# Sigmoid attention feeding a gated two-layer MLP: another opening, and the table of steps that goes with it

## The chip, the core and the metric

The kernel runs on one core of a Trainium2 chip. A core has engines that run side by side, each through its own list of instructions in order: TensorE (PE; its weight loads are shown as PEld) for matmuls, VectorE (DVE), ScalarE (ACT), GpSimd (POOL) and SyncE (SP). Engines wait for one another through semaphores. Transfers between the chip's main memory and the core's on-chip memory are issued by an engine and carried out by 16 DMA engines. Matmul results go to PSUM, eight banks of accumulators, from which VectorE or ScalarE must take them before a bank is used again. The metric is the time of one execution on the device, in microseconds (us).

## The reference

Two layers follow one another. Attention with a sigmoid in place of a softmax, over 8 images of 448 tokens with 12 heads of 64, and then an MLP over all 3,584 tokens with 768 channels and 2,048 hidden units:

```python
scores = scale * np.matmul(q, k.transpose(0, 1, 3, 2)) - np.log(S)
attn = 1.0 / (1.0 + np.exp(-scores))
x = np.matmul(attn, v)            # then heads side by side: (3584, 768)
h = x @ w_in
g = h * (1.0 / (1.0 + np.exp(-beta * h)))
out = g @ w_out
```

## The kernel before

**Tiling.** The 12 heads of an image are done in three groups of four heads (`QPB` = 3), so there are 24 groups; group `g` belongs to image `g // 3`. Queries and keys of a group are loaded as fp32 and cast to fp16 by the transfer (`load_one`, line 129), into one of three buffers called homes; `RAW_HOMES` (line 65) names the home of each group in the order of loading, `OUT_HOMES` (line 66) the homes of result tiles. VectorE turns queries and keys (`transpose`, line 212): one instruction for queries, two for keys. TensorE computes scores with 32 channels at a time in four strips of its array (`score`, line 236), ScalarE takes the sigmoid out of PSUM (`weigh`, line 248), TensorE multiplies by v in two halves of its columns (`attend`, line 302), and VectorE casts the result to the token tile `xT` (line 335).

**MLP.** Hidden units are computed as matmuls of 128 x 128 weights with 224 or 448 tokens. For image 0 the first units are computed one by one (`dense1`, line 348); the rest, and all of the later images, in seven products per block of a scheme that needs seven multiplications for eight (`wino1`, line 463), with sums of weights (`weight_sum`, line 424) and of tokens (`token_sum`, line 443) made by VectorE. The second layer does the same over pairs of token tiles (`wino2`, line 565; sums of hidden units by `hidden_sum`, line 552). GpSimd multiplies part of the hidden units by their sigmoid (`weigh_right`, line 524, and `weigh_below`, line 534).

**The order is written out by hand.** `OPENING` (line 773) and `STEPS` (line 707) are lists of steps that `follow` (line 695) carries out one after another, and every engine gets its instructions in that order. The letters are keys of `RUN` (line 656). Those that the change and the prediction speak of:

- `lG.r.s` loads half `s` of the queries (`r` = 0) of group G; `kG` its keys; `QG` both, whole; `vB` and `KB` load v of image B; `wC` loads piece C of eight of w_in (256 hidden units), `oC.H` a quarter of w_out. All of these are DMAs that GpSimd issues, on one queue; at most eight are outstanding, since each uses one of eight semaphores again.
- `rG.s` turns half `s` of a group's queries, `RG.0` all queries, `RG.1` the keys; `b` turns beta; `EB` copies the last rows of v within the chip. VectorE does these.
- `hG.s.p` is a half visit: scores of half `s` of the queries with the first (`p` = 0) or second half of the keys, and their sigmoids. `VG.j` is a whole visit. `yG.s` and `zG.s` are the two stages of the attend of a half, `AG` the attend of a group.
- `fD` is unit block D of image 0 for the first half of the tokens, `D0.D` for the second half; `IB.d.p` is product p of the seven for image B; `Xb.i` token sums, `Si.p` and `Ti.p` weight sums; `GB.d` and `BB.d.j` are GpSimd's products.
- `Ot.h.p` and `Ut.p.x` are pieces of the second layer, `Ht.i` sums of hidden units.
- `iN` is N matmuls on zeros that fill TensorE while it waits at the start.

Where the next attend is nearer than the next visit, dense matmuls are issued as two of 64 columns instead of one of 128 (`tiled`, line 702). A visit needs score tiles in PSUM that ScalarE has emptied: three exist up to step `p0`, two behind it. Four banks serve everything else, the one least lately used first (`bank`, line 107).

Ahead of `OPENING` come the loads of group 0's first half of queries and its keys on SyncE's queue, ten fill matmuls, and the turns of these (lines 785 to 848).

Of the kernel before, what the change touches and what calls it, by code (L numbers as in the profile page):

```python
# [13 lines left out]
def kernel(  # L14
# [680 lines left out]
    def follow(steps):  # L695
# [26 lines left out]
        U2.5.0 X2.0 U2.5.1 A8 V9.1 K4 U2.3.0 H4.0 U2.3.1 H4.1 U4.1.0 R11.0 U2.7.0 V9.2  # L722
        U4.1.1 R11.1 U2.7.1 U4.6.0 U4.6.1 Q13 V9.0 E3 U2.4.0 U2.4.1 H4.2 R10.0 H4.3 R10.1
        U4.5.0 U4.2.0 U4.5.1 U4.2.1 X2.1 X2.3 U4.7.0 U4.7.1 U4.3.0 X2.2 V10.0 U4.3.1 I2.0.6
        U4.4.0 U4.4.1 A9 V10.3 I2.0.5 R12.1 I2.0.2 I2.1.1 I2.1.6 I2.0.3 V10.1 I2.1.2 I2.0.7
        I2.1.5 G2.0 I2.1.7 I2.0.4 I2.1.3 V10.2 I2.1.4 Q15 G2.1 R13.1 I2.2.1 B2.0.0 I2.2.6
        A10 B2.1.0 B2.0.1 V11.0 I2.2.2 B2.1.1 I2.2.5 R13.0 I2.2.7 I2.3.1 I2.2.3 V11.1 I2.2.4
        B2.2.0 I2.3.6 B2.2.1 I2.3.5 G2.2 I2.3.2 I2.3.7 U6.1.0 I2.3.3 V11.2 I2.3.4 R12.0 X3.0
        U6.1.1 B2.3.1 A11 B2.3.0 V12.2 X3.1 H6.0 U6.2.0 H6.1 Q14 U6.2.1 X3.3 I3.0.1 V12.0
        H6.2 I3.0.6 E4 X3.2 G2.3 I3.0.5 U6.6.0 R15.1 U6.6.1 H6.3 V12.1 U6.5.0 U6.5.1 I3.0.2  # L730
        I3.0.7 V12.3 I3.0.3 U6.3.0 R14.0 I3.0.4 U6.7.0 U6.7.1 U6.3.1 A12 B3.0.1 R15.0 B3.0.0
# [148 lines left out]
```

## Time and profile before

| | us |
|---|---|
| three runs, median | 366.39 |
| lowest and highest of the three | 365.99, 366.56 |
| the profiled execution, on the same scale | 367.32 |
| its span, first to last instruction | 365.6 |
| TensorE busy in the span | 358.9 |
| VectorE busy | 279.6 |
| ScalarE busy | 250.5 |
| GpSimd busy | 168.9 |

All rows of the profile that follow come from that one execution. Times are counted from the start of its span. A row of the timeline has start, length, engine, line, operation, output tile `<-` input tiles, shapes, a count of merged instructions, and in brackets the idle time of that engine before it with what ended it. A matmul's length includes the time until its results have drained, so the distance from one start to the next is the better measure of what a step costs TensorE. The granted clock of TensorE was 1.000 over the span.

### The profile page before, as it was taken

The page shows a single profiled execution, that of the slowest core. Times are in us where ns is not written, and L with a number is a line of the kernel's source. Part 1 is how long each engine was busy: PE and PEld are TensorE (multiplying, and loading weights), DVE is VectorE, ACT ScalarE, POOL GpSimd, SP SyncE. Part 2 cuts the span into 40 slices and gives each one's busy share as a digit, 9 for nine tenths or more (in the row PEclk, how much of TensorE's full clock was granted, in tenths as well). Part 3 has the DMA queues.
Part 4 walks back from the last instruction along what each step waited for, and adds up shares of the span by engine and source line. Part 5 has one row for each costly group of instructions (what it writes and reads, how often), then busy time and mean ns, then how long its engine had stood idle before and what let it go on. Part 6 is the DMA issues. An engine that isn't in the chain of part 4 may idle for free.

```text
span 365.6 us, 9439 instructions
## 1 busy us (share of the span) xinstructions
PE 358.9 (98%) x3819; PEld 241.0 (66%) x3819; DVE 279.6 (76%) x528; ACT 250.5 (69%) x414; POOL 168.9 (46%) x204
## 2 busy tenths in 40 slices
PE   7989999999999999999999999999999999999996
PEld 2568654587456785676766676657855688878564
DVE  5439969999977789776787876778768568888755
...
DMA  8999999930995213153977810694001210110235
GB/s 165 168 198 201 195 204 206 209 61 10 159 180 131 31 23 52 34 105 68 105 123 98 145 45 2 138 127 90 0 4 29 60 45 2 43 29 19 48 81 174
...
## 3 DMA queue, kind: packets, MB, share of 16 engines
...
q1 hardware_dynamic: 6160, 11.71, 12.6%
...
q14 instruction: 14, 0.11, 0.1%
...
## 4 chain that ended last, share of the span: by engine, by line
PE 88%; DMA 6%; POOL 3%; DVE 1%; issue 1%; ACT 0%; POOLq 0%; DVEq 0%; ACTq 0%
PE m_ps L192 70%; PE sco L239 10%; PE av_ps L321 8%; DMA raw<-in_q_dram 3%; DMA raw<-in_k_dram 2%; POOL gt L540 2%; DMA v<-in_v_dram 1%; POOL raw L133 0%; DVE sum L406 0%; POOL gt L530 0%; DVE qT L217 0%; ACT osb L459 0%; DVE v L167 0%; POOL w_in L174 0%; ACT sg L459 0%
## 5 line engine op out<-in xcount | busy, mean ns | idle before, releaser
L251 ACT ACTIVATE attnT<-sco 128x896 f16<-128x896 f32 (+1 forms) x163 | 139.0, 908 | 41.0 <-PE sco L239 40.3
L406 DVE TENSOR_TENSOR osb<-m_ps,osb 128x448 f32<-128x448 f32 (+2 forms) x217 | 127.3, 597 | 49.0 <-PE m_ps L192 35.6
L540 POOL TENSOR_TENSOR gt<-osb,sg 128x448 f16<-128x448 f32 x60 | 68.4, 1157 | 65.3 <-ACT sg L459 65.3
L192 PEld LDWEIGHTS <-w_in 128*128 128x128 f16 (+1 forms) x942 | 76.9, 101 | 14.0 <-issue 7.5
L192 PE MATMUL m_ps<-xT,w_in 128*128 128x224 f16 (+1 forms) x708 | 73.1, 259 | 1.3 <-DMA w_in<-in_moe_w_in_dram 1.2
L530 POOL TENSOR_TENSOR gt<-osb,sg 128x448 f16<-128x448 f32 x30 | 34.5, 1154 | 81.3 <-ACT sg L459 54.1
L459 ACT ACTIVATE sg<-osb,beta_sb 128x448 f32<-128x448 f32 (+1 forms) x120 | 62.5, 576 | 9.3 <-DVE osb L406 8.5
L192 PEld LDWEIGHTS <-sum 128*128 128x128 f16 (+1 forms) x488 | 40.3, 101 | 26.9 <-issue 4.6
L192 PEld LDWEIGHTS <-w_S 128*128 128x128 f16 (+1 forms) x630 | 51.0, 101 | 9.4 <-issue 5.5
L192 PEld LDWEIGHTS <-gt 128*128 128x128 f16 (+1 forms) x434 | 36.2, 100 | 26.3 <-issue 8.5
L192 PE MATMUL m_ps<-w_out,gt 128*128 128x384 f16 (+2 forms) x314 | 53.1, 323 | 0.0
L239 PE MATMUL sco<-qT,kT 32*128 32x448 f16 (+3 forms) x864 | 51.6, 339 | 0.8 <-DVE kT L832 0.5
L192 PE MATMUL m_ps<-xs,w_S 128*128 128x224 f16 (+1 forms) x408 | 42.3, 259 | 0.0
L192 PE MATMUL m_ps<-w_out,sum 128*128 128x384 f16 (+1 forms) x256 | 41.2, 327 | 0.0
L192 PE MATMUL m_ps<-w_T,sum 128*128 128x384 f16 (+1 forms) x232 | 40.4, 326 | 0.2 <-DVE sum L406 0.2
L335 DVE CAST xT<-av_ps 128x448 f16<-128x448 f32 (+1 forms) x54 | 28.2, 564 | 13.2 <-PE av_ps L321 12.9
L321 PE MATMUL av_ps<-attnT,v 128*64 128x448 f16 (+3 forms) x400 | 38.2, 343 | 0.0
L459 ACT ACTIVATE osb<-m_ps,beta_sb 128x224 f32<-128x224 f32 x56 | 22.1, 450 | 16.0 <-PE m_ps L192 10.5
L321 PEld LDWEIGHTS <-v 128*64 128x64 f16 (+1 forms) x432 | 21.2, 108 | 16.8 <-issue 9.5
L239 PEld LDWEIGHTS <-kT 32*128 32x128 f16 (+1 forms) x864 | 13.5, 96 | 22.5 <-issue 19.5
L192 PE MATMUL m_ps<-xT,w_S 128*128 128x224 f16 (+1 forms) x222 | 22.3, 260 | 0.0
L192 PE MATMUL m_ps<-xs,w_in 128*128 128x224 f16 (+1 forms) x234 | 22.1, 260 | 0.0
...
## 6 DMA issues: line engine op xcount, KB each, us to landing
...
raw<-in_k_dram POOLq DMA_DIRECT2D x23, 224.0 KB, 5.2
raw<-in_q_dram POOLq DMA_DIRECT2D x21, 224.0 KB, 3.7
v<-in_v_dram POOLq DMA_DIRECT2D x32, 144.0 KB, 5.9
w_in<-in_moe_w_in_dram POOLq DMA_DIRECT2D x8, 384.0 KB, 11.3
...
v<-in_v_dram POOLq DMA_DIRECT2D x16, 48.0 KB, 6.0
...
```

Of the source, the lines that this page charges most:

```text
L192: nc.tensor.matmul(to[c : c + step], hidden[:, c : c + step], weights, **({} if step == P else {"tile_position": (0, c)}), **flags,)
L239: nc.tensor.matmul(sco[base : base + nk, hh, u0 : u0 + n], kT[g][lo : lo + BLK, jt * P : jt * P + nk, e], qT[g][lo : lo + BLK, c0 : c0 + n ...
L251: nc.scalar.activation(out=at[:, :, 0:n], in_=sco[:, :, 0:n], func=AF.Sigmoid, bias=NEG_LOG_S, scale=MSCALE,)
L321: nc.tensor.matmul(av[hh * D : (hh + 1) * D, 0:n], vs[b][base : base + nk, 2 * (s % NPAIR) + hh, jt], at[base : base + nk, hh, 0:n], start ...
L335: nc.vector.tensor_copy(out=xTs[b][:, s % NPAIR, c0 : c0 + n], in_=av[:, 0:n])
L406: nc.vector.tensor_tensor(out=out, in0=in0, in1=in1, op=op)
L459: nc.scalar.activation(out=out, in_=in_, func=AF.Sigmoid, bias=0.0, scale=beta_sb[:, dc : dc + 1])
L530: nc.gpsimd.tensor_tensor(out=gt[:, 2 * d : 2 * d + 2, off : off + QH], in0=ob[:, 0], in1=sg, op=ALU.mult)
L540: nc.gpsimd.tensor_tensor(out=gt[:, dc, off : off + S].rearrange("p (h n) -> p h n", h=2), in0=oa[:, :, j], in1=sg, op=ALU.mult,)
```

## The change

Three strings of the kernel are replaced; no function is changed. The opening in full:

```diff
-        l1.0.0 h0.0.0 k1 b0 l2.0.0 i4 r1.0 k2 R1.1 h0.0.1 v0 R2.1 l0.0.1 i4 l1.0.1 h1.0.1 i4
-        w0 w1 w2 r2.0 h1.0.0 i2 i2 h2.0.1 E0 w3 i3 h2.0.0 r0.1 y0.0 z0.0 h0.1.0 r1.1 y1.0
-        l2.0.1 z1.0 h0.1.1 y2.0 z2.0 w4 p0 h1.1.0 Q3 w5 f1 f0 f3 r2.1 I0.2.1 h1.1.1 y0.1
-        z0.1 I0.3.1 h2.1.0 y1.1
+        l2.0.0 l0.0.1 h0.0.0 l1.0.0 i4 k2 k1 v0 w2 r1.0 h0.0.1 l1.0.1 r0.1 l2.0.1 i4 r2.0
+        h0.1.0 R2.1 R1.1 w1 w0 i4 h0.1.1 E0 i2 h1.0.1 i2 i2 h1.0.0 y0.0 z0.0 b0 h2.0.0 y0.1
+        z0.1 w3 r1.1 h2.0.1 y1.0 z1.0 p0 h1.1.0 y2.0 z2.0 Q3 I0.2.1 r2.1 f3 h1.1.1 I0.2.2 f1
+        f0 I0.3.1
```

The second half of group 0's queries is the second load of GpSimd's queue (it was the eleventh), ahead of the first half of group 1's queries and ahead of both keys; its two visits come third and fourth, and its attend second. w_in comes in the order 2, 1, 0, 3 and then 4 to 7, with the second halves of groups 1 and 2 behind piece 2 and group 3 ahead of piece 4. There are 28 fill matmuls for 29.

The table of steps holds the same 864 steps with `OPENING`, in another order. Its start, and the stretch from the attend of group 6 to U2.6.0:

```diff
-        R3.0 z1.1 I0.3.2 I0.2.2 w6 h2.1.1 w7 Q4 X0.0 f9 f2 y2.1 z2.1 X0.1 X0.3 f8 D0.10 D0.9
-        R3.1 o0.0 K1 D0.1 D0.0 D0.2 Q5 S1.1 S2.1 V3.1 D0.11 D0.8 D0.3 S3.1 V3.2 I0.2.6
-        I0.2.5 o1.0 V3.3 X0.2 f11 R4.1 R4.0 o0.1 V3.0 S4.1 I0.2.7 Q6 f10 I0.3.6 V4.1 I0.2.3
...
-        A6 V7.1 T3.1 I1.2.1 I1.3.7 X1.3 G1.3 I1.2.6 I1.2.5 Q11 V7.0 I1.3.4 T2.1 I1.2.2
-        B1.3.1 I1.0.1 I1.2.3 B1.3.0 I1.2.7 G1.2 V7.2 I1.0.6 I1.0.5 I1.2.4 R9.0 I1.0.7 I1.0.2
-        B1.2.0 B1.2.1 I1.0.3 I1.1.1 G1.0 I1.0.4 B1.0.0 I1.1.6 B1.0.1 Q10 I1.1.5 I1.1.2
-        I1.1.7 I1.1.3 V8.0 I1.1.4 B1.1.0 T1.1 A7 B1.1.1 V8.1 R9.1 U2.1.0 U2.1.1 H2.0 H2.1
-        I2.0.1 T4.0 Q12 V8.2 U2.2.0 T1.0 U2.2.1 U2.6.0 K3 H2.2 U2.6.1 H2.3 V8.3 G1.1 T4.1
...
-        U26.3.1 U26.4.1 U26.2.0
+        R3.1 w4 h2.1.0 f2 w5 I0.3.2 y1.1 w6 z1.1 h2.1.1 f9 y2.1 z2.1 R3.0 f8 X0.0 D0.0 X0.1
+        w7 X0.3 D0.8 Q4 o0.0 D0.10 D0.1 D0.11 S1.1 S2.1 V3.1 K1 D0.2 D0.9 Q5 o1.0 D0.3 R4.0
+        X0.2 V3.2 I0.2.6 V3.3 S3.1 I0.2.5 f11 V3.0 R4.1 o0.1 S4.1 Q6 I0.2.7 f10 I0.3.6 V4.1
...
+        V6.3 I1.3.3 R8.0 K3 A6 V7.1 I1.3.7 R9.1 I1.2.1 X1.3 I1.2.6 I1.2.5 G1.3 V7.0 R11.1
+        I1.3.4 T2.1 I1.2.2 I1.0.1 B1.3.1 I1.2.3 I1.0.6 G1.2 B1.3.0 V7.2 I1.2.7 I1.0.2 I1.0.5
+        I1.2.4 I1.0.7 B1.2.0 I1.0.3 I1.1.1 I1.0.4 B1.2.1 I1.1.6 B1.0.0 I1.1.5 R8.1 I1.1.7
+        B1.0.1 G1.0 I1.1.2 I1.1.3 V8.0 I1.1.4 Q15 T1.1 R11.0 A7 B1.1.1 B1.1.0 V8.1 U2.1.0
+        U2.1.1 H2.0 H2.1 R9.0 I2.0.1 T1.0 V8.2 U2.2.0 U2.2.1 T4.1 U2.6.0 G1.1 V8.3 U2.6.1
...
+        U26.7.1 U22.4.1 U26.3.0 U26.3.1 U26.4.0 U26.4.1 U26.2.1
```

The strings of homes follow the new order of loading and of results:

```diff
-    RAW_HOMES = "012012012012012102121010"
+    RAW_HOMES = "012021021021202021010210"
```

`OUT_HOMES` is replaced in the same way.

More of the change, by code (lines that the diff above doesn't have):

```diff
@@ L720 @@
-        I1.1.7 I1.1.3 V8.0 I1.1.4 B1.1.0 T1.1 A7 B1.1.1 V8.1 R9.1 U2.1.0 U2.1.1 H2.0 H2.1
-        I2.0.1 T4.0 Q12 V8.2 U2.2.0 T1.0 U2.2.1 U2.6.0 K3 H2.2 U2.6.1 H2.3 V8.3 G1.1 T4.1
[L722 to L731, printed above, removed]
@@ new lines @@
+        O0.0.0 o1.1 V4.2 R5.0 O1.0.1 O0.0.1 O1.0.2 B0.2.0 O0.0.2 I0.3.4 V4.3 Q7 O1.0.3
+        B0.3.0 A4 V5.1 B0.3.1 R6.0 O0.0.3 O0.0.4 O1.0.4 O0.0.5 S2.0 O1.0.5 O1.1.0 X1.0 V5.2
+        O1.1.1 O0.1.0 O1.0.6 K2 O1.0.7 O0.1.1 V5.0 O1.1.2 O0.0.6 O0.1.2 O0.1.3 R6.1 S4.0
+        O0.0.7 O1.1.3 T3.0 V6.2 T2.0 O1.1.4 Q8 O0.1.4 R7.0 Q9 A5 X1.1 V6.1 S3.0 R7.1 O1.1.5
+        O1.1.6 O0.1.5 O1.1.7 O0.1.6 I1.3.1 X1.2 V6.0 Q11 I1.3.6 E2 I1.3.5 O0.1.7 I1.3.2 T3.1
+        V6.3 I1.3.3 R8.0 K3 A6 V7.1 I1.3.7 R9.1 I1.2.1 X1.3 I1.2.6 I1.2.5 G1.3 V7.0 R11.1
@@ new lines @@
+        I1.3.4 T2.1 I1.2.2 I1.0.1 B1.3.1 I1.2.3 I1.0.6 G1.2 B1.3.0 V7.2 I1.2.7 I1.0.2 I1.0.5
+        I1.2.4 I1.0.7 B1.2.0 I1.0.3 I1.1.1 I1.0.4 B1.2.1 I1.1.6 B1.0.0 I1.1.5 R8.1 I1.1.7
+        B1.0.1 G1.0 I1.1.2 I1.1.3 V8.0 I1.1.4 Q15 T1.1 R11.0 A7 B1.1.1 B1.1.0 V8.1 U2.1.0
+        U2.1.1 H2.0 H2.1 R9.0 I2.0.1 T1.0 V8.2 U2.2.0 U2.2.1 T4.1 U2.6.0 G1.1 V8.3 U2.6.1
+        U2.5.0 H2.3 U2.5.1 A8 H4.0 H4.1 V9.1 Q10 U2.3.0 T4.0 X2.0 U4.1.0 U2.3.1 V9.0 U4.6.0
+        U4.1.1 R10.1 H2.2 Q12 U4.5.0 U4.6.1 U4.2.0 U4.2.1 X2.1 E3 R10.0 H4.3 U2.7.0 U4.5.1
@@ new lines @@
+        U2.7.1 H4.2 V9.2 U4.3.0 U2.4.0 X2.3 X2.2 U4.7.0 R12.0 U4.7.1 U4.3.1 V10.0 U2.4.1
+        I2.0.6 U4.4.0 U4.4.1 A9 Q13 V10.3 I2.1.1 I2.0.5 R12.1 I2.1.6 I2.0.2 I2.0.3 G2.0
+        V10.1 K4 I2.1.5 I2.1.7 I2.1.2 I2.0.7 I2.1.3 V10.2 I2.1.4 B2.1.0 I2.0.4 B2.1.1 B2.0.0
+        I2.2.1 A10 V11.0 B2.0.1 I2.2.6 I2.2.5 I2.2.2 R13.0 G2.1 I2.2.7 I2.2.3 I2.3.1 I2.2.4
+        V11.1 B2.2.1 I2.3.2 E4 B2.2.0 I2.3.6 G2.2 I2.3.5 I2.3.7 U6.1.0 I2.3.3 V11.2 I2.3.4
+        B2.3.1 B2.3.0 U6.1.1 A11 K5 R15.1 H6.0 V12.2 H6.1 U6.2.0 I3.0.1 U6.2.1 X3.0 H6.2 Q14
@@ new lines @@
+        V12.0 U6.5.0 X3.1 U6.6.0 X3.2 G2.3 U6.6.1 U6.5.1 R13.1 Q17 I3.0.6 I3.0.2 I3.0.5 H6.3
+        V12.1 X3.3 I3.0.7 I3.0.3 U6.3.0 U6.3.1 V12.3 H8.0 G3.0 I3.1.1 I3.0.4 A12 V13.1 R15.0
+        U6.7.0 I3.1.6 H8.1 U6.7.1 I3.1.2 I3.1.5 V13.0 Q16 R14.1 U6.4.0 R14.0 I3.1.7 U6.4.1
+        I3.1.3 V13.2 I3.1.4 U8.6.0 G3.1 B3.0.1 B3.1.1 U8.1.0 U8.1.1 A13 V14.2 U8.6.1 H8.2
+        I3.2.1 E5 U8.2.0 U8.5.0 U8.5.1 B3.1.0 V14.0 H8.3 I3.2.6 U8.2.1 U8.3.0 B3.0.0 I3.2.5
+        I3.2.2 I3.2.7 I3.2.3 G3.2 V14.1 R16.0 I3.2.4 U8.7.0 I3.3.1 Q18 U8.3.1 B3.2.1 U8.7.1
@@ new lines @@
+        B3.2.0 I3.3.6 V14.3 I3.3.5 U8.4.0 I3.3.7 I3.3.2 U8.4.1 I3.3.3 I3.3.4 X4.0 U10.1.0
+        B3.3.0 U10.1.1 B3.3.1 A14 X4.1 R16.1 H10.0 H10.1 V15.2 U10.2.0 U10.2.1 I4.0.1 X4.2
+        G3.3 I4.0.6 V15.0 I4.0.5 K6 Q19 H10.2 U10.6.0 X4.3 I4.0.2 U10.6.1 H10.3 I4.0.3 V15.1
+        U10.5.0 I4.0.7 G4.0 R17.1 U10.5.1 V16.2 I4.0.4 R18.1 A15 V16.1 U10.3.0 U10.3.1
+        I4.1.1 H12.2 I4.1.6 U10.7.0 V16.0 U10.7.1 I4.1.5 R18.0 I4.1.7 I4.1.2 R17.0 I4.1.3
+        U10.4.0 U10.4.1 H12.0 G4.1 V16.3 I4.1.4 B4.0.1 E6 B4.1.0 I4.2.1 A16 V17.2 B4.0.0
@@ new lines @@
+        I4.2.6 B4.1.1 I4.2.5 I4.2.2 I4.2.7 I4.2.3 V17.0 I4.2.4 I4.3.1 B4.2.1 H12.1 G4.2
+        R19.1 U12.1.0 I4.3.6 U12.1.1 I4.3.5 U12.6.0 Q20 U12.6.1 I4.3.2 Q21 B4.2.0 U12.2.0
+        H12.3 I4.3.7 I4.3.3 V17.1 R19.0 I4.3.4 U12.2.1 B4.3.0 B4.3.1 U12.5.0 U12.7.0 V18.0
+        U12.5.1 G4.3 X5.0 A17 X5.1 Q22 V18.1 U12.7.1 U12.3.0 U12.3.1 X5.3 V18.2 U12.4.0
+        H14.0 I5.0.1 I5.0.6 U12.4.1 H14.1 U14.1.0 I5.0.5 V18.3 I5.0.2 X5.2 U14.1.1 U14.6.0
+        I5.0.3 U14.6.1 R20.0 G5.0 U14.2.0 R21.0 A18 V19.2 H14.2 U14.2.1 I5.1.1 I5.0.7
@@ new lines @@
+        U14.5.0 I5.1.6 H14.3 V19.1 R20.1 U14.5.1 Q23 R21.1 I5.0.4 I5.1.2 I5.1.5 V19.0
+        U14.3.0 I5.1.7 I5.1.3 U14.3.1 I5.1.4 R22.1 U14.7.0 B5.1.1 B5.1.0 U14.7.1 A19 V20.0
+        R22.0 G5.1 I5.2.1 I5.2.6 U14.4.0 I5.2.5 U14.4.1 V20.2 I5.2.2 I5.3.1 B5.0.1 I5.2.3
+        I5.3.6 V20.1 I5.3.5 I5.2.7 I5.3.7 I5.3.2 I5.3.3 G5.2 K7 B5.0.0 I5.3.4 I5.2.4 V20.3
+        R23.1 X6.0 H16.2 B5.2.0 I6.0.1 B5.2.1 A20 V21.2 X6.1 U18.1.0 U18.1.1 U16.1.0 I6.0.6
+        B5.3.0 U16.1.1 B5.3.1 U18.2.0 I6.0.5 R23.0 V21.0 U16.2.0 U16.2.1 I6.0.2 H16.0
@@ new lines @@
+        U18.2.1 H16.1 E7 I6.0.3 V21.1 G5.3 U16.6.0 U16.6.1 U16.5.0 U16.5.1 H18.0 H16.3
+        U16.7.0 V22.0 U16.7.1 A21 H18.1 V22.2 U16.4.0 U16.3.0 X6.2 U16.3.1 V22.1 I6.1.1 X6.3
+        U18.6.0 I6.0.7 U18.6.1 V22.3 U16.4.1 I6.0.4 I6.1.2 I6.1.6 A22 V23.0 U18.5.0 H18.3
+        I6.1.5 U18.5.1 H18.2 G6.0 V23.2 I6.3.1 U18.3.0 I6.1.3 U18.3.1 V23.1 I6.1.7 I6.3.6
+        B6.0.0 U18.7.0 I6.1.4 I6.2.1 B6.1.1 I6.3.2 I6.3.5 A23 B6.0.1 I6.2.6 I6.2.5 I6.2.2
+        B6.1.0 G6.1 I6.3.7 I6.2.7 I6.2.3 I6.3.3 I6.3.4 U18.7.1 G6.3 I6.2.4 I7.1.1 I7.0.1
@@ new lines @@
+        B6.2.1 B6.3.0 U20.1.0 B6.2.0 G6.2 X7.0 I7.3.1 B6.3.1 U18.4.0 X7.1 I7.1.6 I7.0.6
+        U20.1.1 I7.3.6 I7.3.5 I7.1.2 U18.4.1 X7.2 I7.0.5 H20.0 I7.3.2 I7.0.2 H20.1 I7.1.5
+        X7.3 I7.3.3 U20.5.0 U20.2.0 I7.1.3 H20.2 U20.6.0 U22.1.0 I7.1.7 I7.0.3 U20.6.1 G7.1
+        I7.2.1 I7.2.6 G7.0 I7.1.4 I7.2.5 I7.3.7 U20.7.0 U20.5.1 G7.3 H20.3 U20.2.1 I7.3.4
+        B7.3.0 H22.2 U24.1.0 I7.0.7 U22.1.1 B7.1.1 U20.3.0 I7.0.4 B7.3.1 I7.2.7 U20.7.1
+        U20.3.1 I7.2.2 H22.0 B7.1.0 H22.1 I7.2.3 U22.7.0 I7.2.4 U22.5.0 U22.6.0 B7.2.0
@@ L771 @@
+        U22.2.0 B7.0.0 B7.0.1 U24.1.1 U22.6.1 U22.5.1 H24.2 H22.3 U22.7.1 U26.1.0 U20.4.0
+        B7.2.1 U20.4.1 U24.7.0 G7.2 U22.3.0 U22.2.1 H24.0 U22.3.1 U24.2.0 U24.5.0 H24.1
+        U26.1.1 U24.6.0 U24.6.1 U24.5.1 U26.2.0 H24.3 U24.2.1 H26.0 U24.7.1 U22.4.0 U24.3.0
+        H26.1 U24.3.1 U26.6.0 U26.6.1 U26.5.0 U24.4.0 H26.2 U24.4.1 U26.7.0 H26.3 U26.5.1
+        U26.7.1 U22.4.1 U26.3.0 U26.3.1 U26.4.0 U26.4.1 U26.2.1
     """.split()
     OPENING = """
-        l1.0.0 h0.0.0 k1 b0 l2.0.0 i4 r1.0 k2 R1.1 h0.0.1 v0 R2.1 l0.0.1 i4 l1.0.1 h1.0.1 i4
```

49 lines of the change are left out of this document (3 added, 46 removed).

## The prediction

> **What bounds the kernel now.** I read the page first: shares of the engines, the DMA row, the chain of waits.
>
> ```profile
> span 365.6 us, 9439 instructions
> PE 358.9 (98%) x3819; PEld 241.0 (66%) x3819; DVE 279.6 (76%) x528; ACT 250.5 (69%) x414; POOL 168.9 (46%) x204
> ...
> DMA  8999999930995213153977810694001210110235
> ...
> PE 88%; DMA 6%; POOL 3%; DVE 1%; issue 1%; ACT 0%; POOLq 0%; DVEq 0%; ACTq 0%
> ```
>
> TensorE is 98% busy, so a new order of the same matmuls can only move the 6.7 us in which it is idle, and fill. The DMA row is full to about 72 us, and the chain lies 6% on DMA. So I asked next for the engines' busy time by stretch, cut at steps that I place below (columns: stretch, its length, busy time and count of PE, PEld, DVE, ACT, POOL, granted clock, DMA share, GB/s).
>
> ```profile
> 8.98:18.74 9.76, 9.69 (x156) 4.94 (x157) 3.83 (x11) 8.92 (x13) 7.95 (x12) 1.00 1.38 167
> 18.74:28.84 10.10, 8.77 (x140) 6.26 (x140) 3.72 (x11) 8.45 (x17) 4.26 (x6) 1.00 1.37 200
> 28.84:45.03 16.19, 16.15 (x206) 12.62 (x207) 15.84 (x36) 13.95 (x25) 6.61 (x11) 1.00 1.42 199
> ...
> 71.04:87.97 16.93, 16.93 (x192) 14.05 (x190) 15.80 (x28) 15.64 (x30) 9.67 (x10) 1.00 0.30 59
> ...
> 94.20:361.61 267.41, 267.41 (x2748) 182.50 (x2749) 206.95 (x377) 171.39 (x289) 112.58 (x125) 1.00 0.41 71
> ```
>
> From 94.20 on TensorE has no gap in 267.41 us: nothing can be won there, only lost. It loses 1.33 us between 18.74 and 28.84, where it waits for loads, and next to nothing up to 45.03, but there VectorE is busy 15.84 of 16.19: two engines are full at once. Before 18.74 ScalarE is the full one (8.92 of 9.76).
>
> **The opening, and which loads it waits for.** The timeline, for the steps in question (start, length, engine, line, operation; in brackets the idle time before it and what ended it):
>
> ```profile
> 8.34 0.58 DVE L225 STREAM_TRANSPOSE kT<-raw 128x384 f32<-128x384 f32 x1 [0.16 <-DMA raw<-in_k_dram]
> ...
> 8.98 0.70 PE L239 MATMUL sco<-qT,kT 32*128 32x224 f16 x16 [0.24 <-DVE kT L225]
> ...
> 17.64 1.08 PE L321 MATMUL av_ps<-attnT,v 128*64 128x224 f16 x16
> ...
> 18.74 0.58 PE L239 MATMUL sco<-qT,kT 32*128 32x224 f16 x16
> ...
> 19.63 0.83 POOL L174 DMA_DIRECT2D w_in<-in_moe_w_in_dram  x1 [1.27 <-DMA w_in<-in_moe_w_in_dram]
> ...
> 21.39 0.75 PE L192 MATMUL m_ps<-xT,w_in 128*128 128x224 f16 x6 [0.24 <-DMA w_in<-in_moe_w_in_dram]
> ...
> 24.61 0.75 PE L192 MATMUL m_ps<-xT,w_in 128*128 128x224 f16 x6 [0.92 <-DMA w_in<-in_moe_w_in_dram]
> 24.79 0.41 DVE L217 STREAM_TRANSPOSE qT<-raw 128x224 f32<-128x224 f32 x1 [2.27 <-DMA raw<-in_q_dram]
> ...
> 26.88 0.89 POOL L182 DMA_DIRECT2D w_out<-in_moe_w_out_dram  x1 [0.68 <-DMA w_in<-in_moe_w_in_dram]
> ...
> 28.84 1.34 PE L192 MATMUL m_ps<-xT,w_in 128*64 128x224 f16 x24 [0.17 <-DVE xT L335]
> ...
> 29.11 0.61 POOL L153 DMA_DIRECT2D v<-in_v_dram  x1 [0.44 <-DMA raw<-in_k_dram]
> ...
> 31.03 3.63 PE L192 MATMUL m_ps<-xT,w_in 128*128 128x224 f16 x36
> ...
> 34.60 0.57 PE L239 MATMUL sco<-qT,kT 32*128 32x448 f16 x8
> ```
>
> 8.98 is h1.0.1, 17.64 the attend y2.0 and z2.0, 18.74 h1.1.0, 19.63 the issue that w1's landing let go, 21.39 I0.2.1 waiting for w2, 24.61 I0.3.1 waiting for w3, 24.79 the turn of group 2's second half of queries, 26.88 the issue that w4's landing let go, 28.84 f9, 29.11 the issue let go by group 3's keys, 31.03 f8. Six dense steps take 34.60 - 31.03 = 3.57, so one is 0.58 with 0.1 for the change to scores.
>
> All loads go through POOL's one queue and land in their order, and the queue is full. So I place them by KB ahead of them:
>
> ```profile
> raw<-in_k_dram POOLq DMA_DIRECT2D x23, 224.0 KB, 5.2
> ...
> v<-in_v_dram POOLq DMA_DIRECT2D x32, 144.0 KB, 5.9
> w_in<-in_moe_w_in_dram POOLq DMA_DIRECT2D x8, 384.0 KB, 11.3
> ...
> v<-in_v_dram POOLq DMA_DIRECT2D x16, 48.0 KB, 6.0
> ...
> raw<-in_q_dram POOLq DMA_DIRECT2D x5, 112.0 KB, 5.2
> ```
>
> *Up to I0.3.1.* h0.1.0, now third, waits for two turns on VectorE, r1.0 and r0.1, the first of which needs the third load. That ends 336 KB down the queue, where group 1's keys end now: 8.34. Two turns of 0.41 give 9.16, against 8.98 for the third visit today: +0.2. Up to h1.1.0 both orders hold the same eight half visits and three attends at ScalarE's pace, so it starts near 18.9. The four turns of beta now stand between casts; they and the two fills dropped or moved lie in the same stretch. From there to I0.3.1 the new order has h1.1.0, y2.0, z2.0, I0.2.1, f3, h1.1.1, I0.2.2, f1, f0: five dense steps (2.9), two visits (0.58 each) and an attend (18.74 - 17.64 = 1.1), together 5.2, ending near 24.0. w3 ends 3,216 KB down (336 of half queries, 448 of keys, 672 of v, 384 + 224 + 1,152), which is where the second half of group 2's queries ends today: 24.79. So I0.3.1 starts at 24.8 against 24.61, +0.2, and up to 0.8 us lost ahead of it costs nothing.
>
> *From I0.3.1 to f9.* The steps are those of today with f2 in the place of I0.2.2, one dense step for another: 28.84 - 24.61, less the 0.17 of waiting, is 4.06, so 28.86. f9 needs w4, which ends at 4,048 KB, where group 3's keys end today; POOL's row at 29.11 comes some 0.2 behind the landing, so 28.9. f9 starts at 28.9 against 28.84, but today f2 still lies behind it: gain 0.58 - 0.06 = 0.52.
>
> *From f9 to A3.* VectorE is full here, and so the gain isn't TensorE's to keep. The rows:
>
> ```profile
> 35.49 0.95 DVE L406 TENSOR_TENSOR w_S<-w_in 128x1536 f16<-128x1536 f16 x1
> ...
> 36.47 0.96 DVE L406 TENSOR_TENSOR w_S<-w_S,w_in 128x1536 f16<-128x1536 f16 x1
> ...
> 37.49 1.32 PE L192 MATMUL m_ps<-xs,w_S 128*128 128x224 f16 x12
> ...
> 45.03 1.61 PE L321 MATMUL av_ps<-attnT,v 128*64 128x448 f16 x16
> 45.84 0.35 DVE L167 COPY v<-v 64x768 f16<-64x768 f16 x1
> ```
>
> I0.2.6 (37.49) starts as S2.1 ends (37.43). The turn of group 3's keys now stands on VectorE ahead of f2's product, I0.3.2's product and y1.1's two casts, and waits for a load that lands near 26.9; behind the casts y2.1 waits for its PSUM banks. For a gain speaks that f2's product and a paired one no longer lie behind f9; against it that VectorE then waits for f9's sigmoid, which w4 sets. The bounds are 0 (VectorE gains nothing) and 0.52 (TensorE keeps all); no row shows this order, neither end is nearer, and I take the middle, 0.25, for S2.1 and for A3. A3 (45.03) can't use more than some 0.4, since v's copy for image 1 ends at 46.19 and its load keeps its place in the queue.
>
> *To U2.6.0.* The one later stall of size:
>
> ```profile
> 89.32 0.59 POOL L133 DMA_DIRECT2D raw<-in_q_dram  x1
> ...
> 90.45 2.24 POOL L540 TENSOR_TENSOR gt<-osb,sg 128x448 f16<-128x448 f32 x2
> ...
> 92.52 1.47 PE L192 MATMUL m_ps<-w_out,gt 128*128 128x384 f16 x8
> ...
> 93.45 0.69 DVE L406 TENSOR_TENSOR sum<-sum,gt 128x1024 f16<-128x1024 f16 x1
> ...
> 94.20 1.47 PE L192 MATMUL m_ps<-w_T,sum 128*128 128x384 f16 x8 [0.21 <-DVE sum L406]
> ```
>
> 94.20 - 92.52 is 1.68 for two half steps that take 1.3 elsewhere: 0.38 lost to POOL's products of image 1. On POOL as many stand in that run as before, with one pair of load issues in it (Q15 for Q10). Q15 waits for R8.1, but V8.0 needs that turn too and precedes I1.1.4, so it holds up no product. The run starts one dense step earlier relative to TensorE (I1.0.2 is moved ahead of I1.2.4) and without R9.0's turn beside it. I take 0.2 of the 0.38; bounds 0 and 0.38.
>
> *The rest.* One change from dense steps to scores fewer over the table (62 for 63): 0.05 to 0.1. The last steps swap P2's halves; each ends in one add and one store, so 0. Homes of buffers are renamed; their waits are loads' and hidden while the DMA row is not the bound.
>
> Sum: 0.25 + 0.2 + 0.05 = 0.5 off a span of 365.6. The profiled execution took 367.32 with 1.7 outside the span, 0.93 above the median 366.39; nothing outside the span is touched, so **365.9**.
>
> **The rivals.**
> *The load's lost time falls elsewhere.* w2 came 21.39 - 19.4 = 2.0 behind w1 (POOL's row at 19.63, less 0.2), but w3 took 24.61 - 21.39 = 3.2, so some 1.2 was lost to something passing. If it isn't lost ahead of w3 and w4 next time, TensorE goes on at 24.0, and f9 0.8 earlier; VectorE lets 0.4 to 0.8 of that through, so 0.6: 365.3. If as much is lost again ahead of w4, f9 waits, and by the same share the time is 366.6. The Trainium skill, page DMA: Bandwidth & Descriptors, section on why a DMA increments its semaphore by 16, says that a load has landed only when all sixteen engines have done their part. By that rule a single engine held up would delay w3 and each load behind it, the new order included, and the 365.9 stands; the trace shows w4's issue 2.3 behind w3's row, no catching up, and so agrees.
> *Nothing arrives.* VectorE gives nothing before A3, and POOL's run still ends last at U2.6.0: 366.4. For it speaks that VectorE has 0.35 idle in 16.19; against it that the same products are done earlier.
> *VectorE is crowded between A6 and A7* (70.9 to 87.97): the slower one. The new order puts R9.1, R11.1, R8.1 and R11.0 there and takes R9.0 and T3.1 out. By these rows
>
> ```profile
> L217 DVE STREAM_TRANSPOSE qT<-raw 128x448 f32<-128x448 f32 (+1 forms) x27 | 16.6, 614 | 4.5 <-DMA raw<-in_q_dram 4.4
> ...
> L225 DVE STREAM_TRANSPOSE kT<-raw 128x384 f32<-128x384 f32 x23 | 13.1, 568 | 1.2 <-DMA raw<-in_k_dram 1.2
> L229 DVE STREAM_TRANSPOSE kT<-raw 128x64 f32<-128x64 f32 x23 | 4.6, 202 | 0.0
> ```
>
> and S1.1's 0.95, of T3.1's size, that is 3 x 0.77 + 0.61 - 0.61 - 0.95 = 1.36 more, against 16.93 - 15.80 = 1.13 idle. If that idle time can be used, 0.23 is left over, and A7 to A8, with fewer turns, takes it up. If none can, V8.0 waits for R8.1, three dense steps ahead of it, and U2.6.0 for its sums: 365.9 + 1.36 = 367.2. It decides from about 0.7 of waiting on.
>
> **How the numbers follow.** Forecast 0.45, time lost elsewhere 0.22, nothing arrives 0.16, VectorE crowded 0.17. 0.2% is 0.73 us, about what a measurement of this kernel can tell from no change, so faster begins under 365.66. The forecast's own range is 365.4 to 366.4; 0.12 of its 0.45 lies under 365.66 and 0.02 above 367.1. Of the lost time's 0.22, 0.18 is faster, 0.02 slower. The crowded case is slower for 0.15. Faster 0.30, slower 0.19, within 0.2% 0.51. The range takes in the bounds of the terms (0.5 more, 0.5 less) and reaches to the ends of the two rivals: 364.9 to 367.2.
>
> **What would show it.** h0.1.0 near 9.1 behind r0.1; I0.3.1 waiting for w_in up to 24.8 (wrong if TensorE is still computing then); f9 near 28.9 on w4 with f2 done; VectorE full from 30 to 45 and S2.1 ending within 0.3 of 37.3; A3 at 44.6 to 45; no gap ahead of U2.6.0. Gaps of TensorE behind VectorE's turns between 71 and 94, or any beyond 94, would make the prediction wrong to the slow side; w3 landing before 24 to the fast one.

## The result, and the profile after

The changed kernel is slower: 367.79 us median (367.13 to 368.73, 10 runs) against 366.49 (365.99 to 366.97, 10 runs), ratio 1.0036 with a 95% interval of 1.0024 to 1.0047. That is above the forecast range of 364.9 to 367.2.

The two pages do not show it. The profiled execution of the changed kernel took 367.18, the second fastest of its ten, and that of the kernel before took 367.32, above all ten of its timed runs (of 94 more that were timed beside the experiments, 12 took that long or longer). The page of the changed kernel:

```profile
span 365.4 us, 9444 instructions
PE 358.8 (98%) x3824; PEld 240.0 (66%) x3824; DVE 279.9 (77%) x528; ACT 249.8 (68%) x414; POOL 170.7 (47%) x204
...
DMA  9999999972467707750529215613270320101235
...
PE 88%; ACT 4%; DVE 3%; POOL 2%; issue 1%; DMA 1%; SPq 0%; DVEq 0%; ACTq 0%; POOLq 0%
```

The share of DMA in the chain of waits fell from 6% to 1%, and VectorE and ScalarE have come into it. The busy times by stretch say more (changed kernel, cut as before: the third half visit, here h0.1.0; h1.1.0, f9, A3; A6 to A7; U2.6.0 to the last step):

```profile
8.77:18.64 9.87, 9.59 (x155) 4.91 (x155) 3.47 (x12) 9.22 (x14) 7.36 (x11) 1.00 1.52 190
18.64:27.70 9.06, 9.00 (x156) 7.00 (x157) 4.34 (x12) 8.54 (x17) 3.62 (x6) 1.00 1.38 200
27.70:43.91 16.21, 15.55 (x196) 12.04 (x196) 15.37 (x35) 13.81 (x24) 6.82 (x11) 1.00 1.40 199
69.62:86.88 17.26, 17.20 (x196) 14.26 (x194) 16.63 (x33) 16.09 (x30) 10.46 (x12) 1.00 0.63 101
93.12:361.53 268.41, 267.96 (x2749) 181.98 (x2749) 207.92 (x375) 170.64 (x289) 112.57 (x121) 1.00 0.39 68
```

The second row is the gain of these two executions: TensorE is busy 9.00 of 9.06 us where it had 8.77 of 10.10. The last row is the loss: from U2.6.0 to the last step the same matmuls take 268.41 us, and took 267.41. Finer stretches of the same kernel find where:

```profile
200.00:214.00 14.00, 13.87 (x159) 10.34 (x158) 11.74 (x21) 12.14 (x21) 6.04 (x5) 1.00 0.20 45
...
260.00:280.00 20.00, 19.94 (x197) 11.83 (x194) 15.50 (x27) 15.54 (x26) 11.79 (x13) 1.00 0.36 37
...
340.00:345.00 5.00, 4.74 (x30) 2.67 (x29) 4.79 (x6) 0.36 (x2) 4.25 (x4) 1.00 0.00 0
```

The times from one start to the next put names to them, against 0.575 for a dense step and 0.65 for a half step: I4.2.7 (209.70) is followed by I4.2.3 at 210.56, 0.29 late; U16.1.0 (266.39) by I6.0.6 at 267.27, 0.23 late; U24.7.0 (342.23) by U22.3.0 at 343.31, 0.43 late; two small ones add 0.14. The table in the old order has none of these.

To see through the scatter, the profiled executions are cut at A3 and U2.6.0; eight of the 16 are shown. The columns are the lengths of the stretches in us, from starts of steps in the timelines, and the median of the timed runs with its ratio to the kernel before (the kernels e1 to e14 follow below). The runs come from five rounds on different chips, in which the kernel before had medians between 366.43 and 366.88, so medians of different rounds are better compared by their ratios.

| kernel | to A3 | A3 to U2.6.0 | of it A6 to A7 | U2.6.0 to the last step | median | ratio |
|---|---|---|---|---|---|---|
| before | 45.03 | 49.17 | 17.14 | 267.41 | 366.49 | 1 |
| changed | 43.91 | 49.21 | 17.26 | 268.41 | 367.79 | 1.0036 |
| e1: changed opening, old order | 43.73 | 49.09 | 17.14 | 267.38 | 366.05 | 0.9987 |
| e2: old opening, changed order | 44.18 | 49.98 | 17.78 | 268.40 | 367.78 | 1.0036 |
| e4: old, changed ending | 43.81 | 49.23 | 17.14 | 267.92 | 366.60 | 1.0004 |
| e8: e1 with Q10 later | 44.46 | 48.70 | 17.14 | 267.38 | 365.82 | 0.9978 |
| e13: changed, two stalls out | 44.53 | 49.54 | 17.57 | 267.85 | 367.28 | 1.0012 |
| e14: e13 with Q15 later | 43.87 | 49.22 | 17.43 | 267.85 | 366.74 | 1.0003 |

From U2.6.0 on, the length repeats to 0.03 us for one order. The first two columns move by some 0.8 from execution to execution.

### The profile page after: what moved, and what is told of

The parts are those of the page before. It is cut to its first block, busy times and chain, and to the rows that moved or that the text cites. A ratio compares the mean times of both kernels' runs of the same rounds, so it can differ in the third digit from the quotient of the medians.

```text
span 365.4 us, 9444 instructions
## 1 busy us (share of the span) xinstructions
PE 358.8 (98%) x3824; PEld 240.0 (66%) x3824; DVE 279.9 (77%) x528; ACT 249.8 (68%) x414; POOL 170.7 (47%) x204
## 4 chain that ended last, share of the span: by engine, by line
PE 88%; ACT 4%; DVE 3%; POOL 2%; issue 1%; DMA 1%; SPq 0%; DVEq 0%; ACTq 0%; POOLq 0%
PE m_ps L192 67%; PE sco L239 11%; PE av_ps L321 9%; ACT attnT L251 2%; POOL gt L540 2%; DVE sum L406 1%; DMA gt<-in_k_dram 1%; PE idle_ps L812 1%; DVE osb L406 1%; ACT sg L459 1%; DVE xs L406 0%; ACT sg L360 0%; DVE gt L502 0%; POOL raw L133 0%; DVE xT L335 0%
## 5 line engine op out<-in xcount | busy, mean ns | idle before, releaser
L540 POOL TENSOR_TENSOR gt<-osb,sg 128x448 f16<-128x448 f32 x60 | 68.1, 1153 | 47.5 <-ACT sg L459 46.2
L530 POOL TENSOR_TENSOR gt<-osb,sg 128x448 f16<-128x448 f32 x30 | 36.3, 1210 | 88.8 <-ACT sg L459 47.9
L192 PE MATMUL m_ps<-w_T,sum 128*128 128x384 f16 (+1 forms) x240 | 41.3, 327 | 0.2 <-DVE sum L406 0.2
L133 POOL DMA_DIRECT2D raw<-in_q_dram x26 | 15.0, 577 | 22.4 <-DVE qT L217 10.6
```

The source lines that it names most:

```text
L133: nc.gpsimd.dma_start(out=raws[g][:, r, c0:c1].rearrange("p c d -> p (c d)"), in_=(q, k)[r][b, HQ * t : HQ * (t + 1)].rearrange("h (p c) d ...
L192: nc.tensor.matmul(to[c : c + step], hidden[:, c : c + step], weights, **({} if step == P else {"tile_position": (0, c)}), **flags,)
L530: nc.gpsimd.tensor_tensor(out=gt[:, 2 * d : 2 * d + 2, off : off + QH], in0=ob[:, 0], in1=sg, op=ALU.mult)
L540: nc.gpsimd.tensor_tensor(out=gt[:, dc, off : off + S].rearrange("p (h n) -> p h n", h=2), in0=oa[:, :, j], in1=sg, op=ALU.mult,)
```

## The experiments

A step may stand anywhere its inputs allow, so the two tables can be spliced where both have done the same steps. That is so at I0.2.4 (43 us; one fill matmul apart) and nearly so at 285 us.

**e1 and e2: one half from each table.** e1 is the changed table up to I0.2.4 and the old one behind it, e2 the reverse; homes 1 and 2 are exchanged where the order of loading asks for it.

```diff
 ... I0.2.3 I0.2.4
-B0.2.1 E1 G0.2 I0.3.5 A3 V4.0 O1.0.0
...
+E1 I0.3.5 B0.2.0 A3 G0.2 V4.0 I0.3.3
...
```

> The changed table up to I0.2.4 (some 43 us), from there on the old table in its own order, homes 1 and 2 exchanged throughout so that the rest stands as in the kernel before. At I0.2.4 both tables have done the same steps but for one fill matmul. Theory 1, the opening gains and the later order loses: A3 started at 43.91 in the changed kernel's profile against 45.03, so some 1.1 below the kernel before, 365.4, if the old order keeps it all, and no stall of TensorE over 0.2 after 100 us. Theory 2, the old opening's lost load time was an accident of the one execution that was profiled (which took 367.3 where the median is 366.5): the two openings are alike on most executions, and this kernel takes 366.3 to 366.6. Theory 3, the loss comes from the opening by way of the phases of the engines: 367 or more.

> The old table up to I0.2.4, from there on the changed table (the other half of the exchange). Theory 1: the later order loses what the stalls after 94 us add up to and more, so this is the slowest of the four, 367.6 to 368.8. Theory 2: as slow as the changed kernel, 367.6 to 367.9. Theory 3: 366.3 to 366.6, as before.

e1 took 366.05 (365.93 to 366.79), ratio to the kernel before 0.9987 (0.9976 to 0.9998); e2 took 367.78 (367.07 to 368.76), ratio 1.0036 (1.0024 to 1.0048), the changed kernel's own. So the new opening gains some 0.5 with the old order behind it and nothing with the changed one, since e2 is as slow as the changed kernel; and the changed order loses 1.3 behind the old opening and 1.8 behind the new. For the loss, e2 fits theories 1 and 2 alike, and e1, which has only the opening, is not slow: theory 3 is out. For the gain, 366.05 lies between theory 1 (365.4) and theory 2 (366.3 to 366.6): e2 and e4 run the old opening too, and reach A3 at 44.18 and 43.81. The kernel before lost 1.2 us ahead of w3 in the execution that was profiled, where w3 landed at 24.56; in the 15 other traces, e2's and e4's with the same order of loading among them, it landed between 22.55 and 23.34. In e4's, I0.3.1 starts at 23.34, with w3 landed:

```profile
20.74 1.12 PE L192 MATMUL m_ps<-xT,w_in 128*128 128x224 f16 x10
...
23.28 0.56 POOL L133 DMA_DIRECT2D raw<-in_q_dram  x1 [1.42 <-DMA w_in<-in_moe_w_in_dram]
...
23.34 0.75 PE L192 MATMUL m_ps<-xT,w_in 128*128 128x224 f16 x6
```

No trace of the changed opening has that wait: from h1.1.0 to A3 ten executions with it, among them those of e1, e3, e5, e6, e8 to e10, e13 and e14, took 25.26 to 25.28. With the old opening the stretch took 26.29 (before), 25.23 (e2) and 24.94 (e4). Without the wait the old opening is no slower there. So the new one is worth, most likely, that wait; how many of the timed runs had it is not known, since they have no trace.

The row of e1 from U2.6.0 to the last step shows the old order without a gap of TensorE, though it runs 1.4 us earlier; below it e2's, with the changed order:

```profile
92.82:360.20 267.38, 267.38 (x2748) 182.50 (x2749) 206.98 (x377) 171.26 (x289) 112.41 (x125) 1.00 0.41 71
```

```profile
94.16:362.56 268.40, 267.95 (x2749) 181.97 (x2749) 207.68 (x375) 170.64 (x289) 112.64 (x121) 1.00 0.39 68
```

**e3 and e4: the ending alone.** e3 is the changed table up to I6.0.7 and the old ending, e4 the old table up to I6.1.1 and the changed ending; results behind the cut get homes anew.

> The changed table up to I6.0.7 (some 285 us), the rest in the old order. The changed kernel's profile has 0.43 of a stall at U24.7.0 (342 us) and 0.09 at I7.1.3; the old order has none there. If the late loss sits in this last fifth: about 0.5 below the changed kernel, 367.3 or less. If it sits between 45 and 285 us: 367.8 still, with stalls near I4.2.7 (210 us), U16.1.0 (266 us) and V21.1 (273 us) as before.

> The old table up to I6.1.1 (some 285 us), the rest in the changed order. If the loss sits in the last fifth: 0.5 or more above the kernel before, 367.0, with a stall at U24.7.0 behind VectorE's sums, which run beside GpSimd's products. If it sits ahead of 285 us: 366.5 and no such stall.

e4 took 366.60 (ratio 1.0004, 0.9991 to 1.0017), and its trace has the stall of 0.41 at U24.7.0 and 0.09 at I7.1.3: its last stretch is 0.5 longer than the old order's. The time, with its wide interval, does not show these 0.5; the trace does. By it half of the fixed loss sits in the last fifth, and half, by the other two stalls, ahead of it. In e3 (369.26) those two stalls are there as well, but a new one of 1.9 at I6.3.5 hides what the old ending gives:

```profile
302.25 0.53 ACT L491 COPY osb<-m_ps 128x448 f32<-128x448 f32 x1 [2.46 <-DMA out_dram<-osb]
302.81 1.35 DVE L406 TENSOR_TENSOR osb<-m_ps,osb 128x448 f32<-128x448 f32 x2 [1.84 <-ACT osb L491]
302.83 0.77 PE L192 MATMUL m_ps<-xT,w_in 128*64 128x224 f16 x12 [1.72 <-ACT osb L491]
```

ScalarE's copy of a result waits for the store that still reads its home, and TensorE for the copy. That is the price of homes chosen for the splice, not of the old ending; e3 says nothing on the last fifth.

**What makes the largest late stall.** Around U24.7.0 in the changed kernel, VectorE and GpSimd:

```profile
340.02 2.68 POOL L540 TENSOR_TENSOR gt<-osb,sg 128x448 f16<-128x448 f32 x2
340.32 1.39 DVE L406 TENSOR_TENSOR sum<-gt 128x1024 f16<-128x1024 f16 x1
...
341.63 1.61 DVE L406 TENSOR_TENSOR sum<-gt,sum 128x1024 f16<-128x1024 f16 x1
...
342.23 0.81 PE L192 MATMUL m_ps<-w_T,sum 128*128 128x384 f16 x4
342.67 1.58 POOL L530 TENSOR_TENSOR gt<-osb,sg 128x448 f16<-128x448 f32 x1
343.17 1.01 DVE L406 TENSOR_TENSOR osb<-m_ps,osb 128x384 f32<-128x384 f32 x2
...
343.31 0.82 PE L192 MATMUL m_ps<-w_out,sum 128*128 128x384 f16 x4 [0.26 <-DVE sum L406]
...
344.11 0.69 DVE L406 TENSOR_TENSOR sum<-gt 128x1024 f16<-128x1024 f16 x1
```

A sum of two tiles in SBUF takes 0.69 alone and 1.39 and 1.61 beside GpSimd's products; a product, 1.13 alone, takes 1.58 where a sum is under way. The additions that take one input from PSUM (343.17, two in 1.01) are not touched. The two engines take turns, and U22.3.0 waits for the second sum, H22.3, which stands behind H24.2, the sum that U24.7.0 just ahead needs. The profile names a cause for the stall at U16.1.0 too, the slow X6.1:

```profile
265.52 1.24 POOL L160 DMA_DIRECT2D v<-in_v_dram  x2
...
265.87 1.34 DVE L406 TENSOR_TENSOR xs<-xT,xs 128x672 f16<-128x672 f16 x1
...
267.27 0.50 PEld L192 LDWEIGHTS <-w_S 128*128 128x128 f16 x6 [0.45 <-DVE xs L406]
```

For I4.2.7 it names none, and the cause stays open.

**e5, e6, e9, e10: repairs in bundles.** e5 has three edits, e6 a fourth:

```diff
-I4.2.2 I4.2.7 I4.2.3 V17.0 I4.2.4
+I4.2.2 I4.2.7 V17.0 I4.2.3 I4.2.4
...
-H24.2 H22.3 U22.7.1 U26.1.0 U20.4.0 B7.2.1 U20.4.1 U24.7.0 G7.2 U22.3.0 U22.2.1
+H22.3 H24.2 U22.7.1 U26.1.0 U20.4.0 B7.2.1 U20.4.1 U22.3.0 U22.2.1 U24.7.0 G7.2
...
-Q23 R21.1
+Q23 K7 R21.1
...
-G5.2 K7 B5.0.0
+G5.2 B5.0.0
```

> The changed kernel with its three late stalls taken out one by one: V17.0 put ahead of I4.2.3, as the old order has it; K7, the six loads of the last image's v, put behind Q23 (245 us in place of 263), away from X6.1; U22.3.0 and U22.2.1 put ahead of U24.7.0 and H22.3 ahead of H24.2, so that the sum that is needed first runs first. Theory A, each stall is its own and hides nothing: 0.29, 0.23 and 0.42 are gone from the trace, X6.1 on VectorE takes 0.5 in place of 1.34, and the time falls by 0.9: lowest 366.2, median 366.9. Theory B, VectorE and GpSimd have too little room in the later order, and what is taken out at one place comes back at the next: the stalls shift and the time stays within 0.3 of 367.8.

> As e5, and in addition R6.0, the turn of group 6's queries, moved from ahead of S2.0 and X1.0 to behind V5.2. Theory A: in the executions that are slower than the best, R6.0 waits for its load, S2.0 and X1.0 come late behind it and run beside GpSimd's product, both are held up, and all up to 97 us is late. Without it the stall of 0.38 at O1.0.7 is gone in every execution: median 0.4 to 0.6 under that of e5, and within 0.3 of this kernel's own lowest. Theory B, the spread between executions comes from elsewhere (the loads themselves): median as e5.

e5 took 368.91 and e6 369.23, both slower than the changed kernel. The first two edits did what they should (0.29 down to 0.06, 0.43 down to 0.10). K7 did harm: behind its loads four stores landed 6.3 us after their issue (median), in the changed kernel after 2.2, and ScalarE waited for the home that they read. In e5:

```profile
v<-in_v_dram POOLq DMA_DIRECT2D x4, 144.0 KB, 7.2
out_dram<-osb SPq DMA_DIRECT2D x4, 96.0 KB, 6.3
```

```profile
255.45 0.53 ACT L491 COPY osb<-m_ps 128x448 f32<-128x448 f32 x1 [2.11 <-DMA out_dram<-osb]
...
256.03 1.20 PE L192 MATMUL m_ps<-xT,w_in 128*128 128x224 f16 x10 [1.55 <-ACT osb L491]
```

X6.1 met a product instead and took 1.35, so that U16.1.0 loses 0.62 in place of 0.23. In e6 the stall of 0.38 at O1.0.7 that e2 and e3 have is not there; but it is also missing from the changed kernel's own trace and from e13's, where R6.0 stands in its old place, so e6 does not show that moving R6.0 helped. In e2 the chain is: R6.0 waits 0.80 for its load, X1.0 comes late behind it and meets a product (1.44 for 0.50, 1.57 for 1.13), TensorE waits for the product:

```profile
55.13 0.65 DVE L217 STREAM_TRANSPOSE qT<-raw 128x448 f32<-128x448 f32 x1 [0.80 <-DMA raw<-in_q_dram]
...
56.04 1.57 POOL L540 TENSOR_TENSOR gt<-osb,sg 128x448 f16<-128x448 f32 x1 [1.26 <-ACT sg L459]
...
56.53 1.44 DVE L406 TENSOR_TENSOR xs<-xT 128x672 f16<-128x672 f16 x1
...
57.67 0.66 PE L192 MATMUL m_ps<-w_out,gt 128*128 128x384 f16 x3 [0.21 <-POOL gt L540]
```

And e6 still lost 0.28 at I1.2.3 and 0.22 at V7.2, so R6.0 isn't the whole of the middle's scatter.

e9 leaves K7 in place and moves U16.1.1 and U18.2.0 ahead of I6.0.6; e10 adds R6.0 behind V5.2, R11.1 behind H4.1 and Q15 behind B1.1.0.

> As e5, but K7 stays where the changed kernel has it, and the wait of I6.0.6 for X6.1 is covered instead: U16.1.1 and U18.2.0 go ahead of I6.0.6. Theory A, each late stall is its own: the stalls at I4.2.7 (0.29), U16.1.0 (0.23) and U24.7.0 (0.42) are gone, X6.1 is as slow as before, and the time is the changed kernel's less some 0.85: lowest 366.3, median 366.9. Theory B, what is taken out comes back at the next place: 367.5 or more.

> As e9, and in addition three steps of VectorE and GpSimd between 45 and 97 us go out of the way: R6.0 behind V5.2 (as in e6), R11.1 (0.77 of VectorE between X1.3 and I1.3.4's add) behind H4.1, Q15's two load issues behind B1.1.0. Theory A, the crowd on VectorE between 70 and 80 us and these issues make up what the changed order still loses in most executions: the stalls at I1.2.3 and V7.2 are gone, that at U2.6.0 is gone or halved, median 366.0 to 366.4, close to e1. Theory B, the spread comes from the loads: median within 0.2 of e9's.

e9 took 368.35: the two good edits held, but the place at 266 us now loses 1.5 in place of 0.23: U18.2.0 waits for GpSimd's product, which ran beside X6.1, and I6.0.5, behind I6.0.6, for a VectorE addition. e10 took 372.69. Its stretch from A3 to U2.6.0 is 48.90 us, the shortest of any kernel with the changed order, and A6 to A7 is back at the old order's 17.14. Of the three steps that points at R11.1: e6 moves R6.0 and e14 Q15, and they have 17.62 and 17.43. But Q10 loads into the home that R11.1 empties, and waited for it:

```profile
101.52 0.59 POOL L133 DMA_DIRECT2D raw<-in_q_dram  x1 [5.10 <-DVE kT L229]
...
106.69 0.58 DVE L225 STREAM_TRANSPOSE kT<-raw 128x384 f32<-128x384 f32 x1 [3.29 <-DMA raw<-in_k_dram]
```

**e13 and e14: the edits that worked, alone.** e13 is the changed kernel with the first two edits of e5; e14 moves Q15 as well:

```diff
-I1.1.4 Q15 T1.1 R11.0 A7 B1.1.1 B1.1.0 V8.1
+I1.1.4 T1.1 R11.0 A7 B1.1.1 B1.1.0 Q15 V8.1
```

> The changed kernel with two edits alone: V17.0 ahead of I4.2.3, and H22.3 ahead of H24.2 with U22.3.0 and U22.2.1 ahead of U24.7.0. In e5 and e9 these two stalls were gone, but edits beside them cost more than they brought. If each stall is worth what the trace shows: 0.29 + 0.42 less the 0.06 and 0.10 left in e9, so 0.55 under the changed kernel, median 367.25. If the engines behind them set the pace anyway: 367.8.

> As e13, and Q15's two load issues behind B1.1.0, where e8 moved Q10 in the old order. If they hold up the last products of image 1 here as well, the stall of 0.33 and more ahead of U2.6.0 is gone and the median is 0.3 to 0.6 under e13's, 366.7 to 366.95. If VectorE, which is fuller here than in the old order, sets that wait: as e13.

367.28 (ratio 1.0012, 1.0002 to 1.0022) and 366.74 (ratio 1.0003, 0.9995 to 1.0012): by the ratios, the three edits give back 1.2 of the 1.3 us. The two of e13 show in the trace; the row from U2.6.0 on of e14, which has them too, is 0.56 shorter than the changed kernel's:

```profile
93.09:360.94 267.85, 267.78 (x2748) 182.01 (x2749) 208.17 (x375) 170.71 (x289) 111.92 (x121) 1.00 0.40 70
```

What Q15 adds is not shown. The intervals of e13 and e14 overlap, and the wait ahead of U2.6.0 is 0.19 in e14's trace, no shorter than in e5's (0.18) and e9's (0.17), where Q15 stands in its place.

**e8: the last stall of the old order.** e1 with Q10's two issues behind B1.1.1.

```diff
-B1.0.1 Q10 I1.1.5
+B1.0.1 I1.1.5
...
-A7 B1.1.1 V8.1
+A7 B1.1.1 Q10 V8.1
```

> As e1, with Q10, two load issues of GpSimd (some 1.1 us), moved from between the products of image 1 to behind the last of them. If these issues are what holds up the last products and with them H2.1 and U2.6.0: the stall of 0.38 ahead of U2.6.0 is gone, median 365.7. If the products wait for ScalarE's sigmoids anyway: 366.05 as e1, with the stall where it was.

365.82 (365.62 to 366.26), ratio 0.9978 (0.9968 to 0.9988): the fastest version of the study, faster than both kernels, though its interval overlaps e1's. GpSimd's last products of image 1 now start with their sigmoids, the issues follow, and U2.6.0 comes 1.31 after U2.2.0 (91.85), with no wait:

```profile
89.18 2.44 POOL L540 TENSOR_TENSOR gt<-osb,sg 128x448 f16<-128x448 f32 x2 [0.45 <-ACT sg L459]
...
91.57 0.59 POOL L133 DMA_DIRECT2D raw<-in_q_dram  x1
91.66 0.69 DVE L406 TENSOR_TENSOR sum<-gt 128x1024 f16<-128x1024 f16 x1
...
91.85 1.48 PE L192 MATMUL m_ps<-w_out,gt 128*128 128x384 f16 x8
...
93.16 1.46 PE L192 MATMUL m_ps<-w_T,sum 128*128 128x384 f16 x8
```

**e7 and e11: is it the order of w_in?** Both are e1 with the parts loaded 0, 1, 2, 3.

```diff
-Q3 I0.2.1 r2.1 f3 h1.1.1 I0.2.2 f1 f0 I0.3.1
+Q3 f1 r2.1 f0 h1.1.1 f3 I0.2.1 I0.2.2 I0.3.1
```

> As e1 (changed opening, old order from 43 us on), but the parts of w_in are loaded 0, 1, 2, 3 as in the kernel before, and the dense steps from h1.1.0 to I0.3.1 stand as f1 f0 f3 I0.2.1 I0.2.2 in place of I0.2.1 f3 I0.2.2 f1 f0. If the order of the parts matters of itself: slower than e1 by 0.3 or more, with TensorE waiting for w_in ahead of I0.3.1. If only the loads ahead of them and the steps between matter (all three parts land before their first step either way): 366.0 to 366.2, as e1.

> As e7 (parts 0, 1, 2, 3), but with I0.2.1 f3 I0.3.1 in a row and I0.2.2 behind f2, so that ScalarE has copied I0.2.1's result out of its bank long before I0.2.2 adds to it. Theory A, e7 lost 1.2 to that copy alone and 0.4 to f1, which needs the casts of z2.0 at once where I0.2.1 does not: 366.4, 0.4 above e1. Theory B, the parts' order as such costs: 367.5 or more again.

367.74 and 367.62, some 1.6 above e1. The order of the parts, with the order of steps that goes with it, is worth that much, but no part of w_in is waited for. I0.2.1 reads only three of the six pairs of heads, so it can run before z2.0's casts are done; f1, in its place, loses 0.36 to them. In e7 I0.2.2 adds to a bank that ScalarE has yet to copy; in e11, where it stands elsewhere, y1.1 waits 0.82 for a bank that a VectorE product (L363) has to empty. One row of each:

```profile
24.46 1.31 PE L192 MATMUL m_ps<-xT,w_in 128*128 128x224 f16 x12 [1.02 <-ACT osb L491]
```

```profile
27.40 0.89 PE L321 MATMUL av_ps<-attnT,v 128*64 128x224 f16 x14 [0.82 <-DVE gt L363]
```

**e12: one more wait of the opening.** e8 with f11 between V3.2 and I0.2.6.

> As e8 (changed opening, old order, Q10 later), and f11 moved from behind I0.2.5 to between V3.2 and I0.2.6, where TensorE waits 0.22 for S2.1 and then 0.46 for ScalarE's sigmoids of V3.2. If these waits are only a matter of order: 0.3 to 0.5 under e8, median 365.4, the rest being lost at A3, which waits for v's second copy. If ScalarE and VectorE set the pace from 30 to 45 us, the wait comes back behind V3.3: 365.8 as e8.

366.37, 0.55 above e8: the two waits at 36 us went, and V3.0 then lost 1.26, first to ScalarE (0.38), then I0.2.7 to S3.1 (0.45). The wait comes back.

## Why the prediction was wrong

**The step that failed** is the term called "the rest". The working says that from 94.20 on "nothing can be won there, only lost", and then sets no price for losing: "the rest" counts the changes from dense steps to scores (0.05) and the swap of the last steps (0). Yet the whole table behind U2.6.0 was new, and its gapless 267.41 us belonged to the old order. The missing term measured 1.00 (268.41 against 267.41), 0.5 of it in the last fifth (e4), 0.56 of it undone by two edits (e13). The prediction did name gaps beyond 94 as a sign that it would be wrong to the slow side.

**Up to I0.3.1.** h0.1.0 was forecast for 9.16 and came at 8.77: the load that was placed at 8.34, by the KB ahead of it, landed at 6.78, and r0.1 was done at 7.51. I0.3.1 was to wait for w3 until 24.8; it started at 23.69 with w3 landed. The 1.2 us lost ahead of w3 was taken as part of the kernel, and it is in one trace of 16. The rival in which the lost time does not come again described this rightly, for the old opening as well as the new.

**To f9 and A3.** f9 came at 27.70, not 28.9, and A3 1.12 earlier, not 0.25. VectorE was busy 15.37 of 16.21, as full as was said, but S2.1's wait moved with the rest (I0.2.6 at 36.35, against 37.49): a full engine that is fed earlier is done earlier. Against other executions of the old opening the gain is smaller; e1 puts it at 0.5 of the median. That this is near the 0.25 of the sum is luck: the sum kept the wait for w3 in both orders and moved a dense step ahead of f9.

**U2.6.0.** Forecast was that 0.2 of the 0.38 would be saved. The changed kernel's profile kept 0.33, and other traces of that order have between 0.17 and 0.39 (e3 0.63), so some executions save the 0.2 and others nothing. The reason given was wrong: the text had Q15 hold up no product, and in the changed kernel the last products start as Q15's issues end:

```profile
88.19 0.62 POOL L133 DMA_DIRECT2D raw<-in_q_dram  x1
...
88.81 0.55 POOL L133 DMA_DIRECT2D raw<-in_k_dram  x1
...
89.37 2.24 POOL L540 TENSOR_TENSOR gt<-osb,sg 128x448 f16<-128x448 f32 x2
```

That such issues cost time at this place is shown by e8, for Q10 in the old order.

**The crowded VectorE** was the rival with the right sign, and its place was right too. From A6 to A7 the old order took 17.14 in all seven traces that have it; this is the kernel before:

```profile
70.83:87.97 17.14, 17.14 (x196) 14.20 (x194) 15.99 (x28) 15.85 (x30) 9.67 (x10) 1.00 0.31 61
```

The changed order took between 17.26 (its own profile, VectorE busy 16.63) and 17.78 (e2), and 17.14 only in e10, which moves R11.1. So the crowd costs 0.1 to 0.6, not the 1.36 of the rival, on top of the fixed 1.00. Together that is 1.1 to 1.6; 1.3 was measured, with whatever the opening gains in it.

**The level.** The profiled execution was 0.93 above the median, and the sum was simply shifted by that. The excess had a place, the wait for w3, which the sum kept on both sides.

What stays open: what R6.0 and the start of the execution add to the middle's scatter (R11.1 rests on one trace), what Q15 costs, why I4.2.7's stall arises, and the 0.23 at U16.1.0, where both repairs that were tried cost more.
